# Moving sums of activations and gated sums into PSUM, three operands through PSUM, and weight preparation in smaller steps

## The chip, the cores and the metric

The kernel runs on one core of a Trainium2 chip. The metric is device time in microseconds (us) of one execution. Five engines matter: PE (TensorE, matmuls; PEld is its weight load), DVE (VectorE), ACT (ScalarE), POOL (GpSimd) and SP (SyncE, which issues the DMAs). SBUF is the on-chip working memory; PSUM is the memory of eight banks that PE writes and that DVE and ACT can read and write.

## The reference, cut to what matters

```
attn = softmax(scale * q @ mean8(k)^T) @ mean8(v)          # 4 x 8 heads, 576 rows
x    = elu(attn_as_rows @ w_in) @ w_out                    # 2304 x 512
P    = 8 rounds of row and column normalisation of exp(x @ w_gate - max)
for e in range(8):
    h   = maximum(x @ w1[e], 0)                            # 2304 x 1024
    out += P[:, e:e+1] * (h @ w2[e])                       # 2304 x 512
```

The change touches the loop over the eight experts, whose two matrix products are 1300 of the 2100 us or more. All is float32.

## The kernel before, in words

Each float32 operand of a matmul is split into a high part (rounded by an ACT copy, `hi`) and a low part (`lo = x - hi`), and a product is three matmuls: hi*hi, hi*lo, lo*hi. Both products of an expert are done by a fast 2x2 block scheme (seven block products where eight are usual), which needs sums and differences of blocks of x, of the weights and of the activations.

**First layer** (`Unit`, lines 791 to 862). A unit is one pair of weight blocks (32 pairs, four an expert) and one third of the tokens; there are 96 units. A unit has seven products of six matmuls, 384 columns wide, in the order 1, 6, (3 of the unit before), 2, 7, 5, 4, into PSUM tiles pa, pb, pc, pd. `read(m)` takes what a product leaves: ACT copies pa to `m1` after product 1; DVE makes `u2` after 6 and `u3` after 7, and `r22` and `r12` after 5 and 4; ACT applies the relu to `r11`, `r22` and `r12`. After product 3, DVE makes the last activation `c` and from it the four sums HS1 to HS4. Product 2 adds to pa, so PE may start it when ACT has copied `m1`; product 3 adds to pc, so PE may start it when DVE has read `r22` out of pc (line 839). Each `keep` is a DMA to the DRAM tile `hid`. Once for each pair, POOL and ACT prepare a later pair's weights (`split_pair`, lines 770 to 781): POOL makes four sums and, behind ACT's casts, three low parts `w`.

**Second layer** (`Pair`, lines 940 to 1012). A pair is an expert and 256 tokens; there are 72, nine an expert. It has seven products of twelve matmuls, 256 columns wide, in the order 0, 1, (6 of the pair before), 2, 3, 4, 5, into poa, pob, poc, pod. `prepare` (lines 927 to 940) splits an operand loaded from `hid` (tile `hl`) into `g0` (high, ACT) and `g1` (low): operands HS3 and H22 (numbers 3 and 5) on POOL, the other five on DVE. It runs three operands ahead of PE. `read` makes sums on DVE, and `gated` adds gate times sum to the output `acc`. In the first eight steps of an expert, `next_weights` (line 1233) prepares the next expert's second weights: POOL makes the block sums T1 to T4 and all low parts, ACT the high parts.

Buffers: `piece` takes one of 13 SBUF buffers, `slot` one of 24 larger ones, `bank` one of the eight PSUM banks. Behind the attention part the program is not in the order in which it is written: a scheduler sets the order on each engine, by its own estimates of durations, and each engine then runs its list in order.

The sums after product 3, as they stand before the change:

```
nc.vector.tensor_add(c, p["c"], self.u2)
nc.vector.scalar_tensor_tensor(self.r22, c, 0.0, self.r22, op0=ALU.max, op1=ALU.add)
nc.vector.scalar_tensor_tensor(c, c, 0.0, self.r11, op0=ALU.max, op1=ALU.subtract)
nc.vector.tensor_sub(self.r11, self.r22, self.r11)
nc.vector.tensor_sub(self.r12, self.r12, self.r11)
```

Of the kernel before, what the change touches and what calls it, by code (L numbers as in the profile page):

```python
# [17 lines left out]
def tile_attention_mlp_moe(  # L18
# [769 lines left out]
    class Unit:  # L788
# [33 lines left out]
        def read(self, m):  # L822
            p = self.bank
            if m == 1:
                self.m1 = self.temp("m1")
                nc.scalar.copy(self.m1, p["a"])  # L826
            elif m == 6:
                self.u2 = self.temp("u2")
                nc.vector.tensor_add(self.u2, p["b"], self.m1)  # L829
            elif m == 2:  # L830
                self.r11 = self.temp("r11")
                nc.scalar.activation(self.r11, p["a"], AF.Relu)
                self.keep(H11, self.r11)
            elif m == 7:
                self.u3 = self.temp("u3")
                nc.vector.tensor_add(self.u3, p["b"], self.m1)
            elif m == 5:
                self.r22 = self.temp("r22")
                nc.vector.tensor_add(self.r22, p["c"], self.u3)  # L839
                nc.scalar.activation(self.r22, self.r22, AF.Relu)  # L840
                self.keep(H22, self.r22)
            elif m == 4:
                self.r12 = self.temp("r12")
                nc.vector.tensor_add(self.r12, p["d"], self.u3)
                nc.scalar.activation(self.r12, self.r12, AF.Relu)
                self.keep(H12, self.r12)
            else:

                c = self.temp("c21")
                nc.vector.tensor_add(c, p["c"], self.u2)  # L850
                nc.vector.scalar_tensor_tensor(
                    self.r22, c, 0.0, self.r22, op0=ALU.max, op1=ALU.add
                )
                self.keep(HS1, self.r22)
                nc.vector.scalar_tensor_tensor(
                    c, c, 0.0, self.r11, op0=ALU.max, op1=ALU.subtract
                )
                self.keep(HS3, c)
                nc.vector.tensor_sub(self.r11, self.r22, self.r11)
                self.keep(HS2, self.r11)  # L860
                nc.vector.tensor_sub(self.r12, self.r12, self.r11)
                self.keep(HS4, self.r12)


    w2s, loaded, prepared, acc = {}, {}, {}, {}
# [7 lines left out]
    ORDER2 = (1, 6, 2, 7, 5, 4, 3)  # L873
    LOADS2 = (range(0, 4), range(4, 7))

    raw2, sums2 = {}, {}

    def load_w2(e):
# [6 lines left out]
                raw2[e, j] = both[:, i]  # L885
                nc.sync.dma_start(both[:, i], rows.rearrange("(f p) d -> p f d", p=P))

    def sum_w2(e, j):

        if j == T3:  # L890
            for half in range(2):
                fs = slice(2 * half, 2 * half + 2)
                t = sums2[e, half] = piece([P, 2, HF], F32, f"t3_{e}_{half}")
                nc.gpsimd.tensor_sub(t, raw2[e, T1][:, fs], raw2[e, B22][:, fs])  # L894
            return
        a, b = {T1: (T1, B11), T2: (B22, T1), T4: (B21, T2)}[j]
        raw2[e, j] = raw2[e, a]
        nc.gpsimd.tensor_sub(raw2[e, j], raw2[e, a], raw2[e, b])  # L898

    def split_w2(e, j, eng):  # L900
        w2s[e, j] = slot([P, 2, NPAIR, HF], F32R, f"w2_{e}_{j}")
        parts = [(slice(0, NPAIR), raw2.get((e, j)))]
        if j == T3:
            parts = [(slice(2 * half, 2 * half + 2), sums2.pop((e, half))) for half in range(2)]
        for fs, x in parts:
            hi, lo = (w2s[e, j][:, l, fs] for l in range(2))
            nc.scalar.copy(hi, x)  # L907
            eng.tensor_sub(lo, x, f32(hi))  # L908
        if j == T4:
            for k in [k for k in raw2 if k[0] == e]:  # L910
                del raw2[k]

    at_chunk2 = [0]

# [14 lines left out]
    def prepare(i):  # L929
        n, j = divmod(i, 7)  # L930
        part = int(j >= LOADS2[1].start)
        x = loaded[n, part][:, j - LOADS2[part].start]
        hi, lo = (piece([P, NPAIR, P], F32R, f"g{l}_{i}") for l in range(2))
        nc.scalar.copy(hi, x)  # L934
        eng = nc.gpsimd if j in (HS3, H22) else nc.vector
        eng.tensor_sub(lo, x, f32(hi))  # L936
        prepared[i] = hi, lo
        if j == LOADS2[part][-1]:
            del loaded[n, part]
            load_hidden()  # L940

    class Pair:
# [26 lines left out]
                        skip_group_check=not first,  # L969
                    )  # L970

        def temp(self, name, n=1):
            return piece([P, n * HF], F32, f"{name}_{self.n}")

        def gated(self, th, y, v):
            gate = gates[:, self.ix[th], self.e : self.e + 1]
# [9 lines left out]
        def read(self, j):  # L986
            m, p = ORDER2[j], self.bank
            if m == 1:
                self.m1 = self.temp("n1")
                nc.scalar.copy(self.m1, p["a"])  # L990
            elif m == 6:
                self.u2 = self.temp("v2")
                nc.vector.tensor_add(self.u2, p["b"], self.m1)
            elif m == 2:
                self.gated(0, self.y(0)[:, 0:HF], p["a"])
            elif m == 7:
                self.u3 = self.temp("v3")
                nc.vector.tensor_add(self.u3, p["b"], self.m1)
            elif m == 5:
                self.c2 = self.temp("c2", 2)  # L1000
                nc.vector.tensor_add(self.c2[:, HF:DM], p["c"], self.u3)
            elif m == 4:
                nc.vector.tensor_add(self.c2[:, 0:HF], p["d"], self.u3)
                self.gated(1, self.y(1), self.c2)
                self.store(1)
            elif m == 3:
                nc.vector.tensor_add(self.u2, p["c"], self.u2)
                self.gated(0, self.y(0)[:, HF:DM], self.u2)
                self.store(0)

        def store(self, th):
# [151 lines left out]
    def need(u):  # L1163
        while not all(k in made for k in CUTS if k[1] == u):
            advance()

    def first_weights(u):

        if u == 0:
            split_w2(0, B11, nc.vector)  # L1170
            split_w2(0, B22, nc.vector)
            for j in (T3, T1, T2):
                sum_w2(0, j)
        elif u == 1:
            del xslots[0]
            load_hidden()
            split_w2(0, T2, nc.gpsimd)
            split_w2(0, B21, nc.vector)
            split_w2(0, T3, nc.gpsimd)
            split_w2(0, T1, nc.gpsimd)  # L1180
            sum_w2(0, T4)
        else:
            del xslots[1]
            load_hidden()
            load_hidden()
            split_w2(0, T4, nc.gpsimd)

    def end_pair(p):
        p.product(6)
# [37 lines left out]
    w1s.clear()  # L1227


    AHEAD = 3  # L1230
    N2 = len(pairs2)

    def next_weights(e, s):

        assert NUNIT * UB == 9
        if s == 0:
            load_w2(e)
        for j in {2: (T3, T1), 4: (T2,), 6: (T4,)}.get(s, ()):
            sum_w2(e, j)
        for j in {1: (B11, B22), 3: (T3, B21), 4: (T1,), 5: (T2,), 7: (T4,)}.get(s, ()):  # L1240
            split_w2(e, j, nc.gpsimd)


    order2 = [(n + (j == 6), (0, 1, 3, 4, 5, 6, 2)[j], n, j) for n in range(N2) for j in range(7)]
# [3 lines left out]
        prepare(next(coming))  # L1248

    def prepare_next():  # L1250
        i = next(coming, None)
        if i is not None:
            prepare(i)

    before = None
    for n in range(N2):
        e, u, s = pairs2[n]
        pair = Pair(n)
        for j in (0, 1, None, 2, 3, 4, 5):
# [4 lines left out]
            else:  # L1264
                if before is not None:
                    prepare_next()
                    end_pair(before)
                if e + 1 < E:
                    next_weights(e + 1, u * UB + s)
        before = pair  # L1270
    end_pair(before)

# [34 lines left out]
```

## Time and profile before

| | us |
|---|---|
| median of 3 runs | 2108.43 |
| lowest, highest | 2106.16, 2108.53 |
| the profiled execution's own time | 2107.28 |
| its span in the profile | 2105.5 |

The profile shows one execution. For each engine it has the busy time, and for an instruction that waited, how long its engine stood idle and which instruction ended the wait. The profiled execution took 2107.28 us, 1.78 more than its span and 1.15 less than the median.

### The profile page before, as it was taken

What the parts mean: (1) busy time and instruction counts of PE and PEld (TensorE: products, weight loads), DVE (VectorE), ACT (ScalarE), POOL (GpSimd) and SP (SyncE); (2) the same over time, 40 slices, a digit from 0 to 9 for tenths busy, and PEclk for the clock granted to TensorE, in tenths of its full rate; (3) what the DMA queues carried; (4) which work ended last, traced back from release to release, by engine and by line L of the source; (5) the groups of instructions that cost most, each with busy time, mean ns of one, the idle gap of its engine ahead of it and who ended that gap; (6) DMA issues with size and microseconds to landing.
All of it is one profiled execution on the core that took longest, in us unless ns stands there. A gap on an engine that the chain in (4) does not pass through costs nothing.

```text
span 2105.5 us, 35466 instructions
## 1 busy us (share of the span) xinstructions
PE 1979.7 (94%) x12717; PEld 1855.2 (88%) x12717; DVE 1593.7 (76%) x2583; ACT 892.5 (42%) x1755; POOL 791.3 (38%) x555
## 2 busy tenths in 40 slices
PE   6899999999999999999999998998989999898999
PEld 4578888888999999999999988998989998898999
DVE  8687978456897777777777777778787878787776
ACT  5664445344423333333333324554444444444443
POOL 6510000100243334333333325655656564646432
PEclk8899999999999999999999999999999999999999
DMA  9322110000555555555565568684848485857592
GB/s 246 83 65 78 54 47 31 11 1 1 172 186 203 208 204 189 206 206 199 197 213 204 190 224 250 169 235 121 235 122 235 134 223 146 217 146 217 145 294 74
DMA packets 440160, 335.82 MB, mean 159 GB/s; under 512 B 25520, under 2 KB 431024, under 8 KB 439984
## 3 DMA queue, kind: packets, MB, share of 16 engines
q1 hardware_dynamic: 439984, 333.56, 51.4%
q8 instruction: 100, 1.64, 0.3%
q14 instruction: 76, 0.62, 0.1%
HBM read 196.62 MB, written 136.84 MB: 158 GB/s over the span
## 4 chain that ended last, share of the span: by engine, by line
PE 71%; DVE 8%; issue 7%; POOL 5%; DMA 3%; ACT 2%; SPq 1%; DVEq 0%; POOLq 0%; ACTq 0%
PE p L650 9%; PE pa L810 9%; PE p L617 9%; PE pb L810 8%; PE pc L810 7%; PE poc L963 6%; PE poa L963 6%; PE pob L963 6%; PE pd L810 4%; PE pod L963 3%; DVE g L936 3%; DMA hl<-hid 2%; POOL w L908 2%; POOL t L894 1%; POOL rv L898 1%
## 5 line engine op out<-in xcount | busy, mean ns | idle before, releaser
L936 DVE TENSOR_TENSOR g<-hl,g 128x512 fp32r<-128x512 f32 x360 | 374.0, 1054 | 61.1 <-ACT g L934 29.6
L934 ACT CAST g<-hl 128x512 fp32r<-128x512 f32 x504 | 294.5, 620 | 192.8 <-PE poc L963 84.4
L936 POOL TENSOR_TENSOR g<-hl,g 128x512 fp32r<-128x512 f32 x144 | 227.8, 1597 | 320.6 <-ACT g L934 295.5
L781 POOL TENSOR_TENSOR w<-rw,w 128x512 fp32r<-128x512 f32 (+1 forms) x96 | 165.7, 1752 | 349.6 <-ACT w L780 281.4
L810 PE MATMUL pc<-xs,w 128*128 128x384 f32 x1152 | 237.0, 340 | 29.1 <-DVE r L839 29.1
L963 PE MATMUL poc<-w,g 128*128 128x256 f32 x1728 | 239.8, 287 | 21.9 <-DVE g L936 21.1
L963 PE MATMUL pob<-w,g 128*128 128x256 f32 x1728 | 238.5, 287 | 13.0 <-DVE g L936 10.1
L963 PEld LDWEIGHTS poc<-w,g 128*128 128x128 f32 x1728 | 222.1, 195 | 27.1 <-DVE g L936 25.0
L963 PE MATMUL poa<-w,g 128*128 128x256 f32 x1728 | 239.3, 289 | 5.0 <-DVE g L936 4.9
L810 PE MATMUL pa<-xs,w 128*128 128x384 f32 x1152 | 235.0, 338 | 6.2 <-ACT m L826 4.5
L963 PEld LDWEIGHTS pob<-w,g 128*128 128x128 f32 x1728 | 222.0, 195 | 16.7 <-DVE g L936 11.7
L810 PEld LDWEIGHTS pc<-xs,w 128*128 128x128 f32 x1152 | 201.3, 189 | 40.1 <-DVE r L839 40.1
L810 PE MATMUL pb<-xs,w 128*128 128x384 f32 x1152 | 231.0, 335 | 0.7 <-DVE u L829 0.7
L963 PEld LDWEIGHTS poa<-w,g 128*128 128x128 f32 x1728 | 224.8, 197 | 7.2 <-DVE g L936 6.4
L650 PE MATMUL p<-h,w 128*128 128x512 f32 (+1 forms) x960 | 218.0, 375 | 0.4 <-ACT h L638 0.4
L810 PEld LDWEIGHTS pa<-xs,w 128*128 128x128 f32 x1152 | 201.8, 189 | 15.8 <-ACT m L826 15.8
L775 POOL TENSOR_TENSOR rw<-rw 128x256 f32<-128x256 f32 x32 | 28.9, 904 | 490.2 <-DMA rw<-in_moe_w_dram 488.5
L810 PEld LDWEIGHTS pb<-xs,w 128*128 128x128 f32 x1152 | 202.4, 188 | 1.1 <-DVE u L829 1.1
L650 PEld LDWEIGHTS p<-h,w 128*128 128x128 f32 x960 | 169.2, 192 | 30.2 <-ACT h L638 0.6
L840 ACT ACTIVATE r<-r 128x384 f32<-128x384 f32 x96 | 50.4, 525 | 300.8 <-DVE r L839 298.7
L617 PE MATMUL p<-xh,w 128*128 128x512 f32 x512 | 172.4, 396 | 0.0
L908 POOL TENSOR_TENSOR w<-rv,w 128x1024 fp32r<-128x1024 f32 x45 | 118.2, 2633 | 66.7 <-ACT w L907 63.3
(148 smaller groups left out, 3119.6 us busy)
## 6 DMA issues: line engine op xcount, KB each, us to landing
hl<-hid SPq DMA_DIRECT2D x504, 256.0 KB, 5.2
hid<-r SPq DMA_DIRECT2D x576, 192.0 KB, 2.0
hid<-c SPq DMA_DIRECT2D x96, 192.0 KB, 1.9
rw<-in_moe_w_dram SPq DMA_DIRECT2D x128, 128.0 KB, 2.8
rv<-in_moe_w_dram SPq DMA_DIRECT2D x32, 512.0 KB, 6.3
raw<-in_moe_w_in_dram SPq DMA_DIRECT2D x16, 512.0 KB, 4.1
raw<-in_moe_w_out_dram SPq DMA_DIRECT2D x16, 512.0 KB, 12.0
vraw<-in_v_dram SPq DMA_DIRECT2D x16, 288.0 KB
```

The costliest lines, as they stand in the source:

```text
L617: nc.tensor.matmul(ps[:, 0:n], wc[:, 0, a, c * P : (c + 1) * P], b[:, c, :], start=c == 0 and m == 0, stop=c == NC - 1 and m == 2,)
L650: nc.tensor.matmul(ps[j][:, 0 : WIDTH[t]], wc[:, 1, a, j * P : (j + 1) * P], h[b], start=f == 0 and m == 0, stop=f == SIZE[g] - 1 and m == 2,)
L775: g.tensor_sub(raw[:, S3], raw[:, A11], raw[:, A21])
L781: g.tensor_sub(w1s[i][1][:, js], raw[:, rs], f32(w1s[i][0][:, js]))
L810: nc.tensor.matmul(self.bank[b], a[:, c, :], x, start=first and c == 0 and n == 0, stop=c == 1 and n == 2, skip_group_check=not first,)
L840: nc.scalar.activation(self.r22, self.r22, AF.Relu)
L894: nc.gpsimd.tensor_sub(t, raw2[e, T1][:, fs], raw2[e, B22][:, fs])
L898: nc.gpsimd.tensor_sub(raw2[e, j], raw2[e, a], raw2[e, b])
L908: eng.tensor_sub(lo, x, f32(hi))
L934: nc.scalar.copy(hi, x)
L936: eng.tensor_sub(lo, x, f32(hi))
L963: nc.tensor.matmul(self.bank[b], h[a][:, f, :], w2s[self.e, j][:, l, f, :], start=first and f == 0 and n == 0, stop=f == NPAIR - 1 and n == 2,
```

## The change

- **Sums of the first layer.** `c`, the sum HS1 and the difference HS2 are made in PSUM (`c` in place in pc, HS2 in a new bank `s2`), so that each DVE operation has one operand in PSUM and one in SBUF. Two ACT copies bring HS1 and HS2 to SBUF, where the DMA takes them. The number of DVE operations stays at five.
- **Gated sums of the second layer.** The sums that `gated` reads are made in PSUM: `c2` becomes a bank `both`, and the sum after product 3 is made in place in poc.
- **Operands.** H11, H12 and H22 are copied whole to a PSUM bank by a second ACT copy, and DVE takes the low part from there. POOL now takes HS2 and HS1. DVE keeps HS3 and HS4 with both operands in SBUF. `prepare` runs four operands ahead.
- **Weights of the second layer.** Sums and splits go in halves (128x512 for 128x1024), by a generator that is advanced one step before each product.

```diff
@@ Unit.read, product 3
-                c = self.temp("c21")
-                nc.vector.tensor_add(c, p["c"], self.u2)
+                c, s2 = p["c"], bank(f"ps_{self.i}_{self.u}")[:, 0:UW]
+                s3 = self.temp("s3")
+                nc.vector.tensor_add(c, c, self.u2)
                 nc.vector.scalar_tensor_tensor(
-                    self.r22, c, 0.0, self.r22, op0=ALU.max, op1=ALU.add
+                    s3, c, 0.0, self.r11, op0=ALU.max, op1=ALU.subtract
                 )
+                self.keep(HS3, s3)
+                nc.vector.scalar_tensor_tensor(
+                    c, c, 0.0, self.r22, op0=ALU.max, op1=ALU.add
+                )
+                nc.vector.tensor_sub(s2, c, self.r11)
+                nc.scalar.copy(self.r22, c)
                 self.keep(HS1, self.r22)
-                nc.vector.scalar_tensor_tensor(
-                    c, c, 0.0, self.r11, op0=ALU.max, op1=ALU.subtract
-                )
-                self.keep(HS3, c)
-                nc.vector.tensor_sub(self.r11, self.r22, self.r11)
+                nc.vector.tensor_sub(self.r12, self.r12, s2)
+                self.keep(HS4, self.r12)
+                nc.scalar.copy(self.r11, s2)
                 self.keep(HS2, self.r11)
-                nc.vector.tensor_sub(self.r12, self.r12, self.r11)
-                self.keep(HS4, self.r12)
@@ weights of the second layer
+    ON_POOL = (HS2, HS1)
+    THROUGH_PSUM = (H11, H12, H22)
+    def weights_ahead(e):
+
+        load_w2(e)
+        for _ in range(8):
+            yield
+        for half in range(2):
+            for j in (B11, B22, T3, B21, T1, T2, T4):
+                if j in (T3, T1, T2, T4):
+                    sum_w2(e, j, half)
+                    yield
+                yield from split_w2(e, j, half, nc.gpsimd)
+                yield
@@ prepare
         nc.scalar.copy(hi, x)
-        eng = nc.gpsimd if j in (HS3, H22) else nc.vector
+        if j in THROUGH_PSUM:
+            y = bank(f"pg{i}").rearrange("p (f t) -> p f t", f=NPAIR)
+            nc.scalar.copy(y, x)
+            x = y
+        eng = nc.gpsimd if j in ON_POOL else nc.vector
         eng.tensor_sub(lo, x, f32(hi))
@@ Pair.read
-                self.c2 = self.temp("c2", 2)
-                nc.vector.tensor_add(self.c2[:, HF:DM], p["c"], self.u3)
+                self.both = bank(f"pc_{self.n}")
+                nc.vector.tensor_add(self.both[:, HF:DM], p["c"], self.u3)
             elif m == 4:
-                nc.vector.tensor_add(self.c2[:, 0:HF], p["d"], self.u3)
-                self.gated(1, self.y(1), self.c2)
+                nc.vector.tensor_add(self.both[:, 0:HF], p["d"], self.u3)
+                self.gated(1, self.y(1), self.both)
                 self.store(1)
             elif m == 3:
-                nc.vector.tensor_add(self.u2, p["c"], self.u2)
-                self.gated(0, self.y(0)[:, HF:DM], self.u2)
+                nc.vector.tensor_add(p["c"], p["c"], self.u2)
+                self.gated(0, self.y(0)[:, HF:DM], p["c"])
@@ the second layer's loop
-    AHEAD = 3
+    AHEAD = 4
     def prepare_next():
+        advance()
         i = next(coming, None)
-                if e + 1 < E:
-                    next_weights(e + 1, u * UB + s)
+                if e + 1 < E and (u, s) == (0, 0):
+                    side.append(weights_ahead(e + 1))
```

The scheduler's order shows what this makes of three places.

DVE in the first layer, before, around product 3 of unit 14_0 (the names end in pair, unit and a running number):

```order
L829 TENSOR_TENSOR u2_14_1_8237<-pb_14_1_8230,m1_14_1_8228 128x384
L850 TENSOR_TENSOR c21_14_0_8245<-pc_14_0_8199,u2_14_0_8164 128x384
L851 SCALAR_TENSOR_TENSOR r22_14_0_8206<-c21_14_0_8245,r22_14_0_8206 128x384
L855 SCALAR_TENSOR_TENSOR c21_14_0_8245<-c21_14_0_8245,r11_14_0_8188 128x384
L859 TENSOR_TENSOR r11_14_0_8188<-r22_14_0_8206,r11_14_0_8188 128x384
L836 TENSOR_TENSOR u3_14_1_8270<-pb_14_1_8230,m1_14_1_8228 128x384
L861 TENSOR_TENSOR r12_14_0_8217<-r12_14_0_8217,r11_14_0_8188 128x384
L839 TENSOR_TENSOR r22_14_1_8279<-pc_14_1_8272,u3_14_1_8270 128x384
L844 TENSOR_TENSOR r12_14_1_8290<-pd_14_1_8283,u3_14_1_8270 128x384
```

The same place now:

```order
L829 TENSOR_TENSOR u2_14_1_8363<-pb_14_1_8356,m1_14_1_8354 128x384
L851 TENSOR_TENSOR pc_14_0_8325<-pc_14_0_8325,u2_14_0_8287 128x384
L852 SCALAR_TENSOR_TENSOR s3_14_0_8372<-pc_14_0_8325,r11_14_0_8314 128x384
L856 SCALAR_TENSOR_TENSOR pc_14_0_8325<-pc_14_0_8325,r22_14_0_8332 128x384
L859 TENSOR_TENSOR ps_14_0_8371<-pc_14_0_8325,r11_14_0_8314 128x384
L836 TENSOR_TENSOR u3_14_1_8399<-pb_14_1_8356,m1_14_1_8354 128x384
L862 TENSOR_TENSOR r12_14_0_8343<-r12_14_0_8343,ps_14_0_8371 128x384
L839 TENSOR_TENSOR r22_14_1_8408<-pc_14_1_8401,u3_14_1_8399 128x384
L844 TENSOR_TENSOR r12_14_1_8419<-pd_14_1_8412,u3_14_1_8399 128x384
```

Nine operations stand in the same order as before; the four that had two operands in SBUF (lines 851, 855, 859 and 861) now have one in PSUM (tiles pc and ps).

POOL in the second layer, before, in pairs 38 and 39, where most of expert 5's weights are prepared (`rv` are raw blocks and their sums, `t3` the sum T3, `w2` low parts of weights, `g1` low parts of operands; operand 7n+j belongs to product j of pair n):

```order
L936 TENSOR_TENSOR g1_269_17866<-hl38_0_17682,g0_269_17865 128x512
L894 TENSOR_TENSOR t3_5_0_17906<-rv5_0_17618,rv5_6_17621 128x512
L894 TENSOR_TENSOR t3_5_1_17908<-rv5_0_17618,rv5_6_17621 128x512
L898 TENSOR_TENSOR rv5_0_17618<-rv5_0_17618 128x1024
L936 TENSOR_TENSOR g1_271_17912<-hl38_1_17725,g0_271_17911 128x512
L908 TENSOR_TENSOR w2_5_3_18049<-t3_5_0_17906,w2_5_3_18049 128x512
L908 TENSOR_TENSOR w2_5_3_18049<-t3_5_1_17908,w2_5_3_18049 128x512
L898 TENSOR_TENSOR rv5_6_17621<-rv5_6_17621,rv5_0_17618 128x1024
L908 TENSOR_TENSOR w2_5_2_18054<-rv5_6_17621,w2_5_2_18054 128x1024
L898 TENSOR_TENSOR rv5_6_17621<-rv5_6_17621 128x1024
L936 TENSOR_TENSOR g1_276_18009<-hl39_0_17826,g0_276_18008 128x512
```

POOL now, for the first halves (pairs 38 and 39):

```order
L960 TENSOR_TENSOR g1_267_18379<-hl38_0_18254,g0_267_18378 128x512
L906 TENSOR_TENSOR t3_5_0_18468<-rv5_0_18207,rv5_6_18210 128x512
L906 TENSOR_TENSOR rv5_0_18207<-rv5_0_18207 128x512
L960 TENSOR_TENSOR g1_270_18471<-hl38_1_18299,g0_270_18470 128x512
L906 TENSOR_TENSOR rv5_6_18210<-rv5_6_18210,rv5_0_18207 128x512
L915 TENSOR_TENSOR w2_5_3_18489<-t3_5_0_18468,w2_5_3_18489 128x512
L915 TENSOR_TENSOR w2_5_2_18531<-rv5_6_18210,w2_5_2_18531 128x512
L915 TENSOR_TENSOR w2_5_4_18598<-rv5_0_18207,w2_5_4_18598 128x512
L906 TENSOR_TENSOR rv5_6_18210<-rv5_6_18210 128x512
L960 TENSOR_TENSOR g1_274_18534<-hl39_0_18401,g0_274_18533 128x512
```

The steps are half as long, but they still stand together: six of them between the low parts of operands 270 and 274. The second halves stand together too, eight steps in a row, between the low parts of operands 288 and 291 in pairs 40 and 41:

```order
L960 TENSOR_TENSOR g1_288_18839<-hl41_0_18709,g0_288_18838 128x512
L906 TENSOR_TENSOR t3_5_1_18856<-rv5_0_18207,rv5_6_18210 128x512
L906 TENSOR_TENSOR rv5_0_18207<-rv5_0_18207 128x512
L906 TENSOR_TENSOR rv5_6_18210<-rv5_6_18210,rv5_0_18207 128x512
L915 TENSOR_TENSOR w2_5_3_18489<-t3_5_1_18856,w2_5_3_18489 128x512
L915 TENSOR_TENSOR w2_5_4_18598<-rv5_0_18207,w2_5_4_18598 128x512
L906 TENSOR_TENSOR rv5_6_18210<-rv5_6_18210 128x512
L915 TENSOR_TENSOR w2_5_1_18664<-rv5_6_18210,w2_5_1_18664 128x512
L915 TENSOR_TENSOR w2_5_5_18729<-rv5_6_18210,w2_5_5_18729 128x512
L960 TENSOR_TENSOR g1_291_18930<-hl41_1_18757,g0_291_18929 128x512
```

ACT at the same place, before (`n1` is the copy of poa that product 2 of pair 41 needs):

```order
L934 CAST g0_286_18253<-hl40_1_18012 128x512
L934 CAST g0_289_18277<-hl41_0_18115 128x512
L990 COPY n1_41_18294<-poa_41_18281 128x256
L934 CAST g0_290_18296<-hl41_0_18115 128x512
```

And now:

```order
L954 CAST g0_286_18858<-hl40_1_18604 128x512
L913 CAST w2_5_3_18489<-t3_5_1_18856 128x512
L913 CAST w2_5_4_18598<-rv5_0_18207 128x512
L954 CAST g0_289_18883<-hl41_0_18709 128x512
L957 COPY pg289_18886<-hl41_0_18709 128x512
L913 CAST w2_5_1_18664<-rv5_6_18210 128x512
L954 CAST g0_290_18905<-hl41_0_18709 128x512
L913 CAST w2_5_5_18729<-rv5_6_18210 128x512
L957 COPY pg292_18952<-hl41_1_18757 128x512
L1014 COPY n1_41_18926<-poa_41_18913 128x256
```

The copy `n1` of pair 41 now stands behind four casts of weights, each of which waits for a POOL sum of the list above; the last of them (`w2_5_5`) needs the sixth POOL step.

## Rows read from the trace of the kernel before

**Rows 1.** The page: busy us, share of the span, instructions of each engine.
```profile
PE 1979.7 (94%) x12717; PEld 1855.2 (88%) x12717; DVE 1593.7 (76%) x2583; ACT 892.5 (42%) x1755; POOL 791.3 (38%) x555
```
**Rows 2.** Windows, second layer's matmuls: stretch, length, PE, PEld busy, granted clock, DMA.
```profile
1285.00:2009.61 724.61, 667.51 (x5292) 655.30 (x5293) 0.97 0.67 186
2009.61:2100.50 90.89, 90.88 (x758) 90.68 (x756) 1.00 0.62 177
```
**Rows 3.** The same view, first layer's matmuls, two units of pair 20.
```profile
1003.24:1011.87 8.63, 7.84 (x44) 7.20 (x44) 1.00 0.73 250
1011.87:1019.15 7.28, 7.28 (x44) 7.28 (x44) 1.00 0.65 236
```
**Rows 4.** Waits of PE's weight loads, 560 to 1240 us: total, times, longest.
```profile
PEld pc L810 <- DVE r L839: 30.8, 30, 1.0
PEld pa L810 <- ACT m L826: 15.8, 30, 1.7
```
**Rows 5.** The same view, 1240 to 1285 us (the end of the first layer).
```profile
PEld pc L810 <- DVE r L839: 8.2, 3, 3.3
```
**Rows 6.** The same view, 1491 to 2009 us.
```profile
PEld poc L963 <- DVE g L936: 20.4, 15, 2.2
PEld pod L963 <- POOL g L936: 12.4, 5, 2.5
```
**Rows 7.** Timeline 999 to 1007.6 us: start, us, engine, line, what, idle before.
```profile
999.01 5.20 POOL L781 TENSOR_TENSOR w<-rw,w 128x768 fp32r<-128x768 f32 x3 [8.77 <-ACT w L780]
...
999.41 2.09 DVE L855 SCALAR_TENSOR_TENSOR c<-c,r 128x384 f32<-128x384 f32 x1
...
1001.53 1.53 DVE L859 TENSOR_TENSOR r<-r,r 128x384 f32<-128x384 f32 x1
...
1003.45 1.18 DVE L861 TENSOR_TENSOR r<-r,r 128x384 f32<-128x384 f32 x1
...
1005.15 0.99 PEld L810 LDWEIGHTS pc<-xs,w 128*128 128x128 f32 x6 [1.04 <-DVE r L839]
...
1006.54 1.01 PEld L810 LDWEIGHTS pa<-xs,w 128*128 128x128 f32 x6 [0.39 <-ACT m L826]
```
**Rows 8.** Lines 829, 855, 936, 980: duration ns minimum/median/maximum, first and last start.
```profile
L829 DVE TENSOR_TENSOR u<-pb,m x96: 540/558/560, 525.8 to 1276.1; 128x384 f32<-128x384 f32 x96
L855 DVE SCALAR_TENSOR_TENSOR c<-c,r x96: 544/558/2096, 538.4 to 1291.1; 128x384 f32<-128x384 f32 x96
L936 DVE TENSOR_TENSOR g<-hl,g x360: 672/683/2868, 1285.4 to 2095.0; 128x512 fp32r<-128x512 f32 x180
L980 DVE SCALAR_TENSOR_TENSOR acc<-poa,gates,acc x63: 467/472/485, 1392.5 to 2095.6; 128x256 f32<-128x256 f32 x63
L980 DVE SCALAR_TENSOR_TENSOR acc<-v,gates,acc x63: 485/977/2174, 1401.8 to 2101.0; 128x256 f32<-128x256 f32 x63
```
**Rows 9.** Groups of instructions by shape: count, busy us, mean ns, idle before.
```profile
L936 DVE TENSOR_TENSOR g<-hl,g 128x512 fp32r<-128x512 f32 x360 | 374.0, 1054 | 61.1 <-ACT g L934 29.6 <-POOL w L908 19.9 <-DMA hl<-hid 11.5
L934 ACT CAST g<-hl 128x512 fp32r<-128x512 f32 x504 | 294.5, 620 | 192.8 <-PE poc L963 84.4 <-PE pob L963 38.4 <-PE poa L963 25.0
L908 POOL TENSOR_TENSOR w<-t,w 128x512 fp32r<-128x512 f32 x16 | 22.5, 1422 | 0.3 <-ACT w L907 0.3
L894 POOL TENSOR_TENSOR t<-rv,rv 128x512 f32<-128x512 f32 x16 | 25.4, 1605 | 15.4 <-DVE u L836 15.4
L990 ACT COPY n<-poa 128x256 f32<-128x256 f32 x72 | 26.8, 372 | 135.6 <-PE poa L963 135.3
```
**Rows 10.** Timeline 1507 to 1530 us, expert 2, at the next expert's weights.
```profile
1509.91 1.60 PE L963 MATMUL poa<-w,g 128*128 128x256 f32 x12
...
1511.35 1.60 PE L963 MATMUL pob<-w,g 128*128 128x256 f32 x12
...
1521.21 1.25 PEld L963 LDWEIGHTS pod<-w,g 128*128 128x128 f32 x10 [2.47 <-POOL g L936]
...
1522.56 2.76 PE L963 MATMUL poa<-w,g 128*128 128x256 f32 x12
```

More of the change, by code (lines that the diff above doesn't have):

```diff
@@ L886, in load_w2, with half_of, sum_w2, split_w2 @@
                 nc.sync.dma_start(both[:, i], rows.rearrange("(f p) d -> p f d", p=P))
-    def sum_w2(e, j):
+    def half_of(x, half):
+        return x[:, 2 * half : 2 * half + 2]
+    def sum_w2(e, j, half):
+        a, b = {T3: (T1, B22), T1: (T1, B11), T2: (B22, T1), T4: (B21, T2)}[j]
         if j == T3:
[L891 to L909, printed above, removed]
+            out = sums2[e, half] = piece([P, 2, HF], F32, f"t3_{e}_{half}")
+        else:
+            raw2[e, j] = raw2[e, a]
+            out = half_of(raw2[e, j], half)
+        nc.gpsimd.tensor_sub(out, half_of(raw2[e, a], half), half_of(raw2[e, b], half))
+    def split_w2(e, j, half, eng):
+        if (e, j) not in w2s:
+            w2s[e, j] = slot([P, 2, NPAIR, HF], F32R, f"w2_{e}_{j}")
+        x = sums2.pop((e, half)) if j == T3 else half_of(raw2[e, j], half)
+        hi, lo = (half_of(w2s[e, j][:, l], half) for l in range(2))
+        nc.scalar.copy(hi, x)
+        yield
+        eng.tensor_sub(lo, x, f32(hi))
+        if j == T4 and half:
             for k in [k for k in raw2 if k[0] == e]:
                 del raw2[k]
+    def weights_ahead(e):
[8 more added lines that the diff above has]
+                yield from split_w2(e, j, half, nc.gpsimd)
+                yield
     at_chunk2 = [0]
@@ L970, in product, with temp @@
                     )
-        def temp(self, name, n=1):
-            return piece([P, n * HF], F32, f"{name}_{self.n}")
+        def temp(self, name):
+            return piece([P, HF], F32, f"{name}_{self.n}")
         def gated(self, th, y, v):
@@ L1165, in need, with split_now @@
             advance()
+    def split_now(j, eng):
+        for half in range(2):
+            run(split_w2(0, j, half, eng))
     def first_weights(u):
         if u == 0:
-            split_w2(0, B11, nc.vector)
-            split_w2(0, B22, nc.vector)
+            split_now(B11, nc.vector)
+            split_now(B22, nc.vector)
             for j in (T3, T1, T2):
-                sum_w2(0, j)
+                for half in range(2):
+                    sum_w2(0, j, half)
         elif u == 1:
@@ L1176, in first_weights @@
             load_hidden()
[L1177 to L1181, printed above, removed]
+            split_now(T2, nc.gpsimd)
+            split_now(B21, nc.vector)
+            split_now(T3, nc.gpsimd)
+            split_now(T1, nc.gpsimd)
+            for half in range(2):
+                sum_w2(0, T4, half)
         else:
@@ L1185, in first_weights @@
             load_hidden()
-            split_w2(0, T4, nc.gpsimd)
+            split_now(T4, nc.gpsimd)
     def end_pair(p):
@@ L1227, in tile_attention_mlp_moe @@
     w1s.clear()
-    AHEAD = 3
+    AHEAD = 4
     N2 = len(pairs2)
[L1233 to L1241, printed above, removed]
     order2 = [(n + (j == 6), (0, 1, 3, 4, 5, 6, 2)[j], n, j) for n in range(N2) for j in range(7)]
```

## The prediction

> **What bounds the kernel now.** I read the page first: PE is busy for 94% of the span and DVE for 76% [rows 1]. PE being busy that much says that there are at most some 126 us to win, and not where. So I went to the two layers that the change touches and measured the pace of PE in each.
>
> In the second layer the last expert prepares no weights for a next one. Its 756 matmuls take 90.89 us at full granted clock; the seven experts ahead of it take 724.61 us, 103.5 each, at 0.97 [rows 2]. Seven at the last one's pace would be 636.2, so 88.4 us are lost, and they are lost only where weights are prepared beside the products. In the first layer a unit takes 7.28 us when nothing waits (42 matmuls, products 1.04 us apart) and 8.63 in one unit of each pair [rows 3]. The waits of PE's weight loads give the sum: from 560 to 1240 us there are 30 waits for the DVE operation that reads `r22` out of pc, 30.8 us, and 30 for ACT's copy `m1`, 15.8 us [rows 4]. At the end of the layer there are 8.2 us more [rows 5].
>
> Why DVE is late shows in the timeline. POOL runs the three low parts of a pair's weights from 999.01 to 1004.21. In that time three DVE operations of 128x384 take 2.09, 1.53 and 1.18 us, and then PE waits 1.04 us for DVE and 0.39 for ACT, which itself was behind DVE [rows 7]. Such an operation alone takes 0.56, so 3.1 us are added. The durations tell which operations suffer. Line 855 (two operands in SBUF) has median 558 ns and maximum 2096; line 829 (one in PSUM) has median 558 and maximum 560 in the same stretch. Line 936 (two in SBUF) goes from 683 to 2868. Line 980 with poa never passes 485, and the same line with a sum in SBUF has median 977 [rows 8]. So a DVE operation with both inputs in SBUF is held while POOL works, and one with an input in PSUM is not. In the second layer it is the same, and there POOL is late too: PE waits for low parts of both engines [rows 6], and after a wait of 2.47 us twelve matmuls take 2.76 us where they took 1.60 [rows 10], which is the granted clock at its lower level, 1.1 us more.
>
> **First layer, part by part.** Of the five DVE operations behind product 3, four had two inputs in SBUF; now none has. Reading PSUM costs 0.56 each [rows 8]. Writing PSUM by DVE is in no row: I take the same 0.56, because reading PSUM and reading SBUF have one median; nothing is to be gained below it, and as upper bound I take three times that, 1.67. The ACT copies from PSUM lie between 0.37 (256 columns) and 0.62 (512 columns) [rows 9]; I take 0.5.
>
> I walk a unit, t from its first product; products end at 1.04, 2.08, ..., 7.28, and I allow 0.2 for a wait to pass. DVE starts each next operation 0.55 on. Product 3 of the unit before ends at 3.12, so `c` is made from 3.3 to 3.85, `s3` to 4.4, HS1 to 4.95, HS2 to 5.5, `u3` to 6.05, HS4 to 6.6, `r22` to 7.15, and `r12` behind product 4 to 8.05. PE needs `r22` read at 9.36, so 2.2 are spare. DVE has 9 x 0.55 = 5.0 of 7.28 us. ACT copies HS1 at 5.5 to 6.0 and HS2 at 6.6 to 7.1, does the two relus to 7.7 and 8.55, and the next `m1` to 9.05; PE needs it at 3.12 of the next unit, 10.4, so 1.35 are spare. What was late was DVE by 3.1 us; nothing is late next, and the 30 pairs give back 30.8 + 15.8 = 46.6 us. If the spare time of ACT were gone, each further us would cost 96 us, once a unit. At the layer's end DVE still splits expert 0's weights with both inputs in SBUF beside POOL; there I give back half of the 8.2, 4.1.
>
> **Second layer, part by part.** For each of 72 pairs DVE has three low parts from PSUM (0.68, as line 936's median), two from SBUF, and gated sums that no longer wait (977 against 472, 63 times [rows 8]). ACT has three more copies of 0.62 in each pair of 10.1 us; with its seven casts and `n1` that is 6.6, and pairs without weights keep their pace. Running four operands ahead costs nothing there.
>
> What is left is weights. POOL's steps of 128x512 take 1.42 us (low part) to 1.61 (sum T3) [rows 9]; I take 1.42, nearest because fewer DVE operations now hold POOL's reads. Products stand 1.44 apart [rows 10].
>
> First clump (pairs 38 and 39, t from pair 38's start): T3's buffer is free when the sums of the pair before are read, some 0.7. Nine POOL steps follow, to the low part of operand 274: 0.7 + 9 x 1.42 = 13.5. PE wants it two matmuls after 11.52, at 11.76. It is late by 1.7 us.
>
> Second clump (pairs 40 and 41, t from pair 40's start): T3 again needs a buffer, which I take to be free when product 3 is done, 7.1. The sixth step ends at 15.6. ACT, held behind it, casts (0.62), copies an operand to PSUM (0.62) and makes `n1` (0.37): 17.3 with the wait. PE wants `n1` for product 2 of pair 41, at 14.4. It is late by 2.9 us, enough for the lower clock after it, 1.1. The low part 291, last in the list, is ready at 7.1 + 9 x 1.42 = 19.9 and wanted at 20.4 in the shifted program; hidden.
>
> Together 5.7 us an expert, 40 for seven; with 3 for the change of layers (an allowance, half of what the first layer's end may keep) 43 remain of 88.4. The gain is 45.
>
> **Sum.** 46.6 + 4.1 + 45 = 96 us, made against the profiled execution: 2107.28 - 96 = 2011. The median lies 1.15 above that execution, so 2012.
>
> [...] The rows above say that a PSUM input costs DVE nothing: 558 ns both ways [rows 8]. [...]
>
> **The rivals.**
> - *The two low parts left in SBUF and POOL's own lateness keep the second layer's loss.* HS3 and HS4 are still held by POOL, and POOL by them. With 1.61 us a step the first clump is late by 0.7 + 14.5 - 11.76 = 3.4, the second by 7.1 + 9.7 + 1.7 - 14.4 = 4.1, and both then have the lower clock: 9.7 an expert, 68 in all. Only 88.4 - 71 = 17 come back: 2040. With nothing back there it is 2108.4 - 50.7 = 2058. For it: the clumps still stand in the order; against it: two such operations a pair where there were six. [...] 21 in 100.
> - *Nearly all waits go.* POOL undisturbed at less than 1.3 a step makes the first clump punctual and the second late by about 2, without the lower clock: 7 x 2 + 3 = 17 remain, 71 come back, with the whole end of the first layer 46.6 + 8.2 + 71 = 126: 1983; without the second lateness 1969. 13 in 100.
> - *The change does nothing it says.* DVE would have to be late for another reason than POOL. The flat line 829 beside POOL's work speaks against it. 2108, 3 in 100.
> - *Slower: DVE's writes to PSUM are so slow that ACT's copies reach `m1` too late in every unit.* Three operations a unit write PSUM. At 1.4 us each (2.5 times) the chain ends 2.55 later, 1.2 beyond the spare 1.35: 96 x 1.2 = 115 us, 2012 + 115 = 2127. It is slower than before from 1.35 us a write on; at 1.67 it is near 2200. For it: no row shows such a write; against it: no PSUM operand in these rows costs more than an SBUF one. 5 in 100.
>
> **How the numbers follow.** Forecast 56, first rival 21, second 13, no change 3, slower 5; 2 for what lies between the first rival and no change. The forecast's own range is 1990 to 2035, from 1.3 to 1.55 us a POOL step and the layer's end at all or nothing. The range reaches to the first rival's end and to the first figure of the second, 1980 to 2060; outside are about half of the second rival, no change, slower and the 2: some 17 in 100. A difference of 0.2% (4 us) is about what a measurement of this kernel can tell. Faster by more: 56 + 21 + 13 + 2 = 92; within: 3; slower: 5.
>
> **What the profile after would show.** The DVE lines behind product 3 have maxima near their medians; PE's waits for `r22` and `m1` in the first layer are gone and every unit takes 7.28. In the second layer waits of about 2 and 3 us remain twice an expert, at product 1 of the fourth pair and at product 2 of the sixth, the second for ACT's `n1`; quiet pairs keep their pace. Wrong would be: DVE operations that write PSUM well above 0.56; waits for `m1` in every unit; waits for a free PSUM bank; or the two clumps late by far more or not at all.

## The result, and the profile after

The changed kernel takes 2032.88 us (median of 4 runs, 2030.57 to 2037.3), the kernel before 2108.01 in the same comparison. The ratio is 0.9648, with a 95% interval of 0.963 to 0.9665. That is 75 us faster, within the forecast range, where the forecast itself was 96.

On the page PE is busy for 96% of a span of 2031.3 us, against 94% in [rows 1]. The windows show where the 75 us come from. First the second layer's matmuls (columns as in [rows 2]): expert 0, experts 1 to 6, expert 7.

```profile
PE 1950.4 (96%) x12717; PEld 1851.9 (91%) x12717; DVE 1360.8 (67%) x2586; ACT 1101.2 (54%) x2211; POOL 725.5 (36%) x624
```
```profile
1235.87:1342.06 106.19, 96.85 (x757) 94.90 (x757) 0.95 0.75 217
1342.06:1935.44 593.38, 561.96 (x4539) 558.48 (x4538) 0.97 0.69 189
1935.44:2026.32 90.88, 90.88 (x758) 90.67 (x756) 1.00 0.59 172
```

An expert at full pace is nine pairs of 10.08 us, 90.72. Experts 1 to 6 take 98.9 each and so lose 8.2, expert 0 loses 15.5: 64.5 in all, where the kernel before lost 89.6 counted in the same way. The second layer gives 25 us.

The first layer ran from 521.8 to 1284.9 us and now runs from 520.6 to 1235.2, so it gives 48.5. The two units of pair 20 that [rows 3] show now take 7.27 and 7.28:

```profile
976.87:984.14 7.27, 7.27 (x43) 7.27 (x43) 1.00 0.79 264
984.14:991.42 7.28, 7.28 (x43) 7.28 (x43) 1.00 0.68 248
```

The last two units of the layer took 25.8 us and take 16.9, so 8.9 of the 48.5 come from there and 39.6 from the units ahead of them. First before, then now:

```profile
1259.07:1284.90 25.83, 17.86 (x85) 16.08 (x84) 0.91 0.65 207
```
```profile
1218.31:1235.20 16.89, 15.28 (x85) 14.33 (x84) 1.00 0.93 292
```

The waits that answer to [rows 4] (PE's weight loads, 560 to 1240 us) were 30.8 and 15.8 us. They are almost gone:

```profile
PEld pa L810 <- ACT m L826: 3.1, 3, 1.2
PEld pc L810 <- DVE r L839: 1.3, 2, 1.1
```

The operations behind product 3 and the first of ACT's two copies, with their durations (ns: minimum, median, maximum), to be read against line 855 in [rows 8], which reached 2096:

```profile
L851 DVE TENSOR_TENSOR pc<-pc,u x96: 548/567/567, 535.6 to 1235.2; 128x384 f32<-128x384 f32 x96
L852 DVE SCALAR_TENSOR_TENSOR s<-pc,r x96: 548/557/559, 536.2 to 1235.9; 128x384 f32<-128x384 f32 x96
L856 DVE SCALAR_TENSOR_TENSOR pc<-pc,r x96: 554/556/556, 536.7 to 1236.4; 128x384 f32<-128x384 f32 x96
L859 DVE TENSOR_TENSOR ps<-pc,r x96: 554/567/567, 537.7 to 1237.0; 128x384 f32<-128x384 f32 x96
L862 DVE TENSOR_TENSOR r<-r,ps x96: 543/545/556, 538.6 to 1240.2; 128x384 f32<-128x384 f32 x96
L860 ACT COPY r<-pc x96: 470/481/485, 538.5 to 1239.7; 128x384 f32<-128x384 f32 x96
```

Minimum, median and maximum of each line lie within 19 ns, so none is held any more. The three lines that write PSUM (851, 856, 859) have medians of 567, 556 and 567 ns, and line 852, which writes SBUF, 557. ACT's copy takes 0.48 us.

In the second layer three waits are left in each of experts 1 to 6 (PE's weight loads, 1342 to 1936 us):

```profile
PEld pob L987 <- POOL g L960: 17.0, 6, 3.1
PEld poa L987 <- ACT n L1014: 11.7, 6, 1.9
PEld poc L987 <- ACT w L913: 6.2, 6, 1.0
```

Windows of pairs of expert 3, from product 1 to product 1, and in the last row the sixth pair of expert 4. They show which pairs lose: 4.33 in the fourth, 1.08 in the fifth, 3.48 or 2.00 in the sixth.

```profile
1559.80:1569.88 10.08, 10.08 (x86) 10.08 (x85) 1.00 0.28 80
1569.88:1584.29 14.41, 11.82 (x86) 11.62 (x85) 0.88 0.26 74
1584.29:1595.45 11.16, 10.30 (x86) 10.12 (x85) 1.00 0.42 125
1595.45:1609.01 13.56, 11.82 (x86) 11.62 (x85) 0.87 0.94 256
1695.44:1707.52 12.08, 10.34 (x86) 10.14 (x85) 1.00 0.93 250
```

The timeline of the first of these waits, read from the top: POOL stands idle for 4.14 us before T3's sum. The profile names nothing that ends this idle time ("issue"); it is taken here to be the wait for a buffer for T3, which is argued and not shown. Then an ACT cast of an operand waits 3.51 us for a POOL step that makes a low part of the weights; that this step sets T3's buffer free is argued too. POOL in turn waits 1.25 us for a cast that stood behind it on ACT. The low part that PE needs starts at 1571.55, PE's weight load waits 2.79 us for it, and the twelve matmuls of the next product take 2.60 us for 1.60. The two rows below them are the wait for `n1`, in experts 3 and 4: PE stands idle for 1.74 us, and its weight load, which ended a little earlier, for 1.94.

```profile
1559.67 1.30 POOL L906 TENSOR_TENSOR t<-rv,rv 128x512 f32<-128x512 f32 x1 [4.14 <-issue]
1566.13 0.62 ACT L954 CAST g<-hl 128x512 fp32r<-128x512 f32 x1 [3.51 <-POOL w L915]
1567.36 2.56 POOL L915 TENSOR_TENSOR w<-rv,w 128x512 fp32r<-128x512 f32 x2 [1.25 <-ACT w L913]
1571.55 1.27 POOL L960 TENSOR_TENSOR g<-hl,g 128x512 fp32r<-128x512 f32 x1
1572.87 1.70 PEld L987 LDWEIGHTS pob<-w,g 128*128 128x128 f32 x10 [2.79 <-POOL g L960]
1574.66 2.60 PE L987 MATMUL poc<-w,g 128*128 128x256 f32 x12
...
1600.23 2.46 PE L987 MATMUL poa<-w,g 128*128 128x256 f32 x12 [1.74 <-ACT n L1014]
...
1699.86 1.70 PE L987 MATMUL poa<-w,g 128*128 128x256 f32 x12 [1.74 <-ACT n L1014]
```

### The profile page after: what moved, and what is told of

It is laid out like the page before. It is cut to its first block, busy times and chain, and to the rows that moved or that the text cites. A ratio compares the mean times of both kernels' runs of the same rounds, so it can differ in the third digit from the quotient of the medians.

```text
span 2031.3 us, 35842 instructions
## 1 busy us (share of the span) xinstructions
PE 1950.4 (96%) x12717; PEld 1851.9 (91%) x12717; DVE 1360.8 (67%) x2586; ACT 1101.2 (54%) x2211; POOL 725.5 (36%) x624
## 5 line engine op out<-in xcount | busy, mean ns | idle before, releaser
L954 ACT CAST g<-hl 128x512 fp32r<-128x512 f32 x504 | 305.2, 620 | 164.0 <-PE pob L987 83.1
L960 POOL TENSOR_TENSOR g<-hl,g 128x512 fp32r<-128x512 f32 x144 | 187.2, 1300 | 335.5 <-ACT g L954 266.0
L781 POOL TENSOR_TENSOR w<-rw,w 128x512 fp32r<-128x512 f32 (+1 forms) x96 | 140.9, 1499 | 327.2 <-ACT w L780 259.1
L987 PEld LDWEIGHTS pob<-w,g 128*128 128x128 f32 x1728 | 227.0, 199 | 18.9 <-POOL g L960 17.9
L810 PE MATMUL pc<-xs,w 128*128 128x384 f32 x1152 | 231.9, 335 | 2.2 <-DVE r L839 2.2
L775 POOL TENSOR_TENSOR rw<-rw 128x256 f32<-128x256 f32 x32 | 23.9, 747 | 507.9 <-DMA rw<-in_moe_w_dram 415.1
L960 DVE TENSOR_TENSOR g<-pg,g 128x512 fp32r<-128x512 f32 x216 | 148.7, 688 | 84.4 <-ACT g L954 39.4
L960 DVE TENSOR_TENSOR g<-hl,g 128x512 fp32r<-128x512 f32 x144 | 117.6, 817 | 38.2 <-ACT g L954 15.4
L829 DVE TENSOR_TENSOR u<-pb,m 128x384 f32<-128x384 f32 x96 | 53.4, 557 | 133.1 <-PE pb L810 65.1
```

Source lines behind the costliest of these rows:

```text
L775: g.tensor_sub(raw[:, S3], raw[:, A11], raw[:, A21])
L781: g.tensor_sub(w1s[i][1][:, js], raw[:, rs], f32(w1s[i][0][:, js]))
L810: nc.tensor.matmul(self.bank[b], a[:, c, :], x, start=first and c == 0 and n == 0, stop=c == 1 and n == 2, skip_group_check=not first,)
L987: nc.tensor.matmul(self.bank[b], h[a][:, f, :], w2s[self.e, j][:, l, f, :], start=first and f == 0 and n == 0, stop=f == NPAIR - 1 and n == 2,
```

## The experiments

Each of the twelve kernels was timed beside the kernel before, whose median in the four groups was 2108.25, 2106.44, 2108.47 and 2109.54 us. "Loss of an expert" is the mean of experts 1 to 6 above 90.72 us in the profiled execution; before it is 12.9, in the changed kernel 8.2. A diff here shows only the lines that matter; `...` marks what is left out.

**1. The parts one by one, each put on the kernel before.** The first layer's hunk of the change alone:

> The kernel before with the first layer's part of the change alone (the five operations behind product 3 with a PSUM operand, the two copies back by ACT). Theory (POOL held the operations with two SBUF inputs, nothing else of the change matters here): the first layer gives back what it gave in the changed kernel, 763.1 - 714.6 = 48.5 us, so 2108 - 48.5 = 2059.5 (2057 to 2062). Rival (the first layer's end was cured by the small weight steps, not by PSUM): some 8 us less, 2064 to 2068.

Measured: 2061.22 us (2060.58 to 2063.48), ratio 0.978 [0.9766, 0.9795]: 47.0 us. The first layer does not need the rest of the change. Its last unit but one takes 11.14 us, the changed kernel's 9.45, so the rest of the change adds less than 2 us there.

The PSUM parts of the second layer alone (the hunks of `ON_POOL`, `THROUGH_PSUM` and `both`), and the small steps alone, with the fourth operand ahead (the hunks of `weights_ahead`, `advance()` and `AHEAD = 4`):

> The kernel before with the second layer's PSUM parts alone (sums and gated sums in PSUM, three operands copied to PSUM for their lows, HS1 and HS2 on POOL), the old weight steps of 128x1024, three operands ahead. Theory A (what the second layer gave back, 25 us, came from DVE no longer being held): 2108 - 20 = 2088 (2083 to 2093). Rival B (it came from the small steps, which let POOL's low parts in between): 2103 (2098 to 2108).

> The changed kernel without its PSUM parts in either layer: only the weights in half steps, one step a product, and four operands ahead. Theory A (DVE's holding was the cost): the held operations stay, so 2103 (2098 to 2108). Rival B (POOL's long steps were the cost): 2088 (2083 to 2093). If both single parts give little and the two together 25, they need each other.

Measured: 2092.16 us (2091.12 to 2093.84), ratio 0.9926 [0.9911, 0.9941], and 2085.98 (2083.21 to 2091.26), ratio 0.9891 [0.9873, 0.991]. Each lies in the range of the theory that it was to test, A for the first and B for the second. So each gives most of the gain alone, 16 and 22 us, and both together only 28 (2061.2 of the first experiment less 2032.9): the two gains overlap. Each edit also lets the scheduler set a new order, which is part of these prices. With PSUM and the long steps one long wait an expert is left, for POOL, up to 7.0 us:

```profile
PEld pob L971 <- POOL g L944: 42.2, 6, 7.0
```

**2. Is it PSUM, or the new order of the five operations?** The changed kernel with the two sums in SBUF buffers:

```diff
-                c, s2 = p["c"], bank(f"ps_{self.i}_{self.u}")[:, 0:UW]
+                c, s2 = self.temp("c21"), self.temp("s2")
 ...
-                nc.vector.tensor_add(c, c, self.u2)
+                nc.vector.tensor_add(c, p["c"], self.u2)
```

> The changed kernel with the first layer's operations in the changed order and with ACT's two copies, but the two sums in SBUF buffers and not in PSUM. Theory (a DVE operation with both inputs in SBUF is held while POOL works): four of five operations have two inputs in SBUF again, PE's waits behind product 3 come back in one unit of each pair, and most of the 47 us are lost: 2070 to 2085. Rival (the new order of the five operations and the copies on ACT gave the gain): 2033 to 2040.

Measured: 2082.02 us (2079.08 to 2084.16), ratio 0.9878 [0.986, 0.9896]. All of the first layer's gain is lost again (49.1 more than the changed kernel). The copies are the same; in units 60 to 62 of the two traces DVE runs the same operations in the same order, and on ACT only the copy of line 860 stands one place earlier. The operations with two SBUF inputs are held again, and the two waits of [rows 4] are back:

```profile
L856 DVE SCALAR_TENSOR_TENSOR c<-c,r x96: 544/558/2091, 535.8 to 1285.1; 128x384 f32<-128x384 f32 x96
L859 DVE TENSOR_TENSOR s<-c,r x96: 499/560/1644, 536.4 to 1285.8; 128x384 f32<-128x384 f32 x96
L862 DVE TENSOR_TENSOR r<-r,s x96: 543/558/1532, 537.5 to 1290.8; 128x384 f32<-128x384 f32 x96
```
```profile
PEld pc L810 <- DVE r L839: 30.5, 29, 1.5
PEld pa L810 <- ACT m L826: 15.6, 29, 2.0
```

In the two traces line 856 reaches 2091 ns with both inputs in SBUF and 556 at most with one in PSUM. What inside the chip makes DVE wait is not shown.

**3. What the second layer still loses.** The loop over the pairs under the order in which the code is written, on all engines, where a scheduler had set it:

```diff
+    with tc.manual_schedule(engines={E_.PE, E_.DVE, E_.Activation, E_.Pool, E_.SP}):
     for n in range(N2):
         ...
```

> The changed kernel with the instructions of all engines in the second layer in the order in which the code writes them; then two weight steps at most stand between two of POOL's low parts, where runs of up to eight stood. Theory (the loss left in the second layer, 8.0 us an expert, comes from those runs in POOL's order and from ACT and PE instructions placed behind them): the loss falls to 2 us or less an expert, 2033 - 6 x 7 = 1991 (1983 to 2000). Rival 1 (POOL has too little time for weights beside products, whatever the order): 2025 to 2040. Rival 2 (reads and low parts in the written order wait for one another): 2045 or more.

Measured: 2003.69 us (2001.67 to 2005.31), ratio 0.9505 [0.949, 0.952]. The loss of an expert falls to 2.8. That is 29 us less than the changed kernel and 13 more than the figure expected (4 above its range); expert 0 still loses 17.5. The waits of the pairs with weights are now ACT's: its casts wait for POOL's sum one step ahead, with `n1` behind them (1346 to 1907 us):

```profile
ACT w L913 <- POOL rv L906: 80.1, 36, 2.9
...
ACT w L913 <- POOL t L906: 21.9, 6, 3.7
```

So the sums (s) were moved three steps or more ahead of their casts (c); l is a low part:

```diff
+    AHEAD2 = "cB11 lB11 sT3 cB22 lB22 sT1 cT3 lT3 cB21 lB21 sT2 cT1 lT1 sT4 cT2 lT2 cT4 lT4".split()
 ...
```

> The kernel with the written order, and each sum of weights made three or more steps ahead of the cast that reads it, where the cast came one step behind. Theory (the 2.7 us an expert that the written order still loses are ACT's casts that wait for POOL's sum, with the copy n1 behind them): the loss goes to 0.6 us or less, 2003.7 - 7 x 2.3 = 1988 (1984 to 1992). Rival (POOL is late in any case, or the longer hold of the buffer of T3 costs as much): 1998 to 2010.

Measured: **1976.08 us** (1975.43 to 1976.84), ratio 0.9376 [0.9361, 0.9391], 12 us better than expected and 57 us faster than the changed kernel. Experts 1 to 6 have no wait of PE left, and PE is busy in all of their time; expert 0 loses 5.8:

```profile
1333.50:1877.80 544.30, 544.30 (x4539) 544.30 (x4538) 1.00 0.76 207
1236.96:1333.50 96.54, 93.37 (x757) 92.66 (x758) 0.98 0.80 226
```

Three kernels ask what this needs. The written order on the kernel before, then the last kernel without the second layer's PSUM parts (`gated` reads SBUF sums again), and with whole weight steps:

```diff
-    ON_POOL = (HS2, HS1)
-    THROUGH_PSUM = (H11, H12, H22)
+    ON_POOL = (HS3, H22)
+    THROUGH_PSUM = ()
 ...
```
```diff
-        return x[:, 2 * half : 2 * half + 2]
+        return x if half is None else x[:, 2 * half : 2 * half + 2]
 ...
```

> The kernel before with the second layer's instructions in the order in which its code writes them, nothing else. Theory (the order helps only small steps that can stand apart; steps of 128x1024 that are written together keep POOL for 5 us and more): 2095 to 2120. Rival (the order was the whole cost of the second layer, and neither small steps nor PSUM are needed): 2030 to 2050.

> The kernel with the written order and the early sums, without the second layer's PSUM parts (lows and gated sums from SBUF, HS3 and H22 on POOL). Theory (operations with two SBUF inputs and POOL hold each other, in a good order too): 4 us or more an expert, 2010 to 2030. Rival (with small steps in this order the PSUM parts give nothing): within 5 us of the kernel with them.

> The kernel with the written order and the early sums, but each weight step over the whole weight again (128x1024; T3, which has no buffer of that size, in two steps of 128x512 written together), one step in two products. Theory (a step of some 2.6 us that stands alone between two low parts is hidden by the four operands of lead, 5.8 us; it was the runs that cost): within 5 us of 1976. Rival (the small steps are needed as such): 2 us an expert or more, 1990 and up.

Measured: 2130.01 us (2127.19 to 2131.69), ratio 1.0103 [1.0082, 1.0124]; 2027.15 (2025.46 to 2028.35), ratio 0.9618 [0.9602, 0.9634]; 1987.5 (1985.68 to 1989.42), ratio 0.943 [0.9414, 0.9445]. The written order alone is slower than what it replaces, and 10 us above the range expected: steps that are written side by side stay side by side, and PE waits for POOL's low parts four times an expert. The PSUM parts are worth 51 us in this order, where they were worth 16 on the kernel before. Without them DVE is late: PE's weight loads wait four times an expert for a DVE sum that reads pob (1340 to 1930 us), where with them there is no such wait. DVE's low parts (line 968) have a median of 0.69 us and reach 1.81; with the PSUM parts, those from PSUM reach 0.69 at most and the others, with two SBUF inputs, 1.83.

```profile
PEld pob L995 <- DVE v L1025: 33.0, 24, 1.5
```

And POOL itself takes longer for steps of the same size. First without the PSUM parts, then with them (POOL, ns):

```profile
L968 POOL TENSOR_TENSOR g<-hl,g x144: 1271/1722/1810, 1238.6 to 2012.0; 128x512 fp32r<-128x512 f32 x144
L915 POOL TENSOR_TENSOR w<-rv,w x90: 1269/1475/1754, 1218.3 to 1903.8; 128x512 fp32r<-128x512 f32 x90
```
```profile
L968 POOL TENSOR_TENSOR g<-hl,g x144: 1286/1298/1684, 1240.3 to 1959.6; 128x512 fp32r<-128x512 f32 x144
L915 POOL TENSOR_TENSOR w<-rv,w x90: 1288/1302/1758, 1220.0 to 1851.7; 128x512 fp32r<-128x512 f32 x90
```

The small steps are worth 11 us: with whole ones an expert loses 0.9 and expert 0 11.9. The figure lies between the two that were expected; the theory holds for experts 1 to 6 (5 us in all) and not for expert 0, whose waits were not taken apart.

**4. What makes the first wait of an expert.** Three kernels in the scheduler's order: the early sums (the list `AHEAD2` of above) without the written order, a pool of their own for T3's sums, and three operands ahead.

```diff
-            out = sums2[e, half] = piece([P, 2, HF], F32, f"t3_{e}_{half}")
+            out = sums2[e, half] = t3pool.tile([P, 2, HF], F32, tag="t3", name=f"t3_{e}_{half}")
 ...
```
```diff
-    AHEAD = 4
+    AHEAD = 3
```

> The changed kernel with the early sums, in the order that it had (not the written one): between two low parts on POOL there now stand up to eight weight steps where the worst run of the fourth pair had four. Theory (the order decides, the early sums help only where the steps stand apart): not faster than the changed kernel, 2033 to 2055. Rival (ACT's wait for the sums is what matters, in any order): 2005 to 2020.

> The changed kernel with a buffer of its own for T3's sums, where they share the pieces of the operands; the order on POOL changes with it, ten weight steps stand in one run. In the changed kernel POOL waits 4.1 us for that shared buffer ahead of the first run, and an ACT cast waits 3.5 us for the step that sets it free. Theory (that wait is what makes the first run late, the length of a run matters less): the first wait of each expert goes, 3 to 5 us each, 2033 - 6 x 4 = 2009 (2003 to 2018). Rival (the length of the run decides): ten steps of 1.27 stand ahead of a low part, 2035 or more.

> The changed kernel with three operands ahead, as before, not four: two buffers more are free, and each operand has 1.44 us less lead. Theory (the shared buffer is the cost): T3 starts earlier, 2015 to 2028. Rival (the lead is what hides the runs): each of the two waits of an expert grows by up to 1.44, 2033 + 6 x 2.9 = 2050 (2040 to 2055).

Measured: 2008.89 us (2007.09 to 2011.02), ratio 0.9531 [0.9517, 0.9545]; 2040.59 (2037.53 to 2041.73), ratio 0.9676 [0.966, 0.9692]; 2008.56 (2008.24 to 2009.17), ratio 0.9523 [0.9509, 0.9537]. Two theories fell here: that the order alone decides (the first kernel), and that the wait ahead of T3 alone does (the second). The early sums give 24 us in the scheduler's order too, though up to seven weight steps stand together: the first run starts earlier, POOL's idle time before T3's sum shrinks from 4.1 us to 0.7, and an expert loses 4.7. With a buffer of its own, T3's sum starts 1 us into expert 3 and not 20, behind a wait of 5.3 us for the DMA of the raw weights, but the run of ten steps behind it then makes one long wait, where ACT's `n1` and then POOL are late (1348 to 1940 us). An expert loses 7.9, nearly the 8.2 of the changed kernel, and the last unit of the first layer takes 15.9 us for 7.4:

```profile
PEld poa L988 <- ACT n L1015: 26.9, 6, 6.1
PEld poc L988 <- POOL g L961: 8.9, 6, 2.5
```

With three operands ahead, two buffers more are free, no operand's cast on ACT waits for a POOL step on the weights, the runs are of five and six steps, and an expert loses 4.4; the time lies 6 us below the range of its theory. Each edit also changes the order on POOL, so the shares of the buffer and of the length of the runs are not separated. That both count fits the three runs and is not shown. Three operands ahead were not tried in the written order.

## Why the prediction was right, point by point

The mechanism was right in the first layer, which gave 48.5 us for 50.7. In the second layer it was right in kind and too hopeful in size: 25 us came back for 45, since 64.5 us remain where 43 were to remain. That is about the 21 us by which the measured 2032.9 misses the forecast 2012. It lies only 2 us inside the forecast's own range, 1990 to 2035.

- **DVE held by POOL, and only with two SBUF inputs: right.** Experiment 2 switches nothing but the place of two sums, and the 49 us come and go with it, as does line 856's maximum, 2091 or 556 ns.
- **First layer, 46.6 + 4.1 = 50.7: right in sum, and there luck helped.** 48.5 in the trace, 47.0 alone. But the units ahead of the last two gave 39.6 for 46.6, and the last two 8.9 for 4.1, so two errors nearly cancel. The first one shows in the rows of before: a late unit is 8.63 - 7.28 = 1.35 us longer [rows 3], while its two waits of weight loads average 1.55 [rows 4]. The sum of those waits is more than what the units lose.
- **A write to PSUM at 0.56, an ACT copy at 0.5: right.** 0.556 to 0.567, and 0.48. The 0.62 that was taken as the upper end for copies from PSUM is the row of a cast from SBUF; nothing hung on it. The slower rival needed 1.35 a write. Nor does an input in PSUM cost DVE more here: line 862 has a median of 545 ns with one input in PSUM and of 558 with both in SBUF (experiment 2).
- **Second run of an expert, late by 2.9, and 1.1 for the clock: right in sum, not in form.** `n1` was ready 17.3 us after the pair's start, as forecast. But PE met the lateness in two parts: 1.04 already in the fifth pair, where two matmuls of the last product had been placed early, and 1.94 in the sixth. Behind 1.94 the granted clock fell only in every other expert (0.87 over the sixth pair of expert 3, 1.00 over that of expert 4). The losses, 1.1 and 2.7, make 3.8, for 4.0 forecast.
- **First run, late by 1.7: mis-sized, and the main error.** It costs 4.3. POOL's steps were cheaper than assumed: the nine took 1.32 us each, from 1559.67 to 1572.82 less POOL's own wait, for 1.42. But T3's sum started 1.3 us after the pair's start for 0.7, and POOL waited 1.25 us for ACT, which itself had waited 3.5 for POOL; the working had no such wait. (The nine are seven weight steps and two low parts. Between the low parts of operands 270 and 274 stand five steps, as in the order listed ahead of the prediction, and not six.) PE wanted the operand at 11.7, as forecast, and got it at 14.5. With a wait of 2.8, not 1.7, came 1.5 us of lower clock (0.58 in the 4 us behind the wait). That is 2.6 more an expert, 16 us in experts 1 to 6, of the 21 that are missing.
- **Four operands ahead cost nothing: right only for the pairs without weights, of which it was said.** They keep their 10.08 us. For the pairs with weights the sum had no such term, and there three are 24 us faster in this kernel, with fewer buffers held and another order on POOL.
- **Change of layers and expert 0, 3 + 5.7: too small.** 15.5; the first pair alone took 16.3 us for 10.1. The 3 was an allowance that no row gives. The 15.5 were not taken apart further than that 10 us of them go with the written order and the early sums together.
- **The first rival** (2040 to 2058) came nearer in time, 7 us off for the forecast's 21, and about as near in the loss of an expert: 9.7 for a measured 8.2, where the forecast had 5.7. It was right that POOL is later and that the lower clock follows the first wait each time (0.57 to 0.62 in the 4 us behind it, in experts 1 to 6). But its reason was another: it priced POOL's steps at 1.61, and in the first run they took 1.32. (Its count of DVE operations with two SBUF inputs, six in a pair before, leaves one out: five low parts and two gated sums are seven.) What it describes is seen without the PSUM parts (experiment 3), where a low part on POOL takes 1.72.

## What to carry to other kernels

Where DVE and GpSimd work side by side, look for DVE operations with two SBUF inputs, and try one of the inputs in PSUM: here that gave 47 us in one layer and 16 to 51 in the other, and in experiment 3 the median of POOL's low part fell from 1.72 to 1.30 us with it, and the longest of the DVE low parts that moved to PSUM is 0.69 us, where DVE's low parts had reached 1.81. Then look at the order of the helper's steps on the engine that runs them: here sums only one step ahead of the cast that reads them made ACT wait, and PE behind it, and sums three steps ahead took 28 us away in the written order. A longer lead also holds more buffers; here the kernel with the fourth operand ahead was 24 us slower in the scheduler's order.

## What the runs showed of the hardware

- Holding went both ways here. POOL's low part of 128x512 has a median of 1722 ns beside DVE operations with two SBUF inputs and 1298 without most of them (experiment 3).
- A wait of 1.94 us ahead of the same product was followed by a granted clock of 0.87 over the pair in expert 3 and of 1.00 in expert 4. Ahead of it the two experts look alike: their fourth pairs took 14.41 and 14.42 us, their fifth 11.16 and 11.17. It went on in turn: the sixth pair took 13.6 us in experts 1, 3 and 5 and 12.1 in experts 2, 4 and 6. Why the clock fell in one and not in the other stays open.
- A DVE operation of 128x384 with one input in PSUM has a median of 556 to 567 ns where it writes PSUM (lines 851, 856, 859) and of 545 to 557 where it writes SBUF (lines 862, 852), in the changed kernel.
